# FFT convolutions of a three-stage SSM chain: the transform regrouped as 128 by 32 points, its products on 64x64 blocks

## The chip, the core and the metric

The kernel runs on one core of one Trainium2 chip. TensorE (PE) multiplies matrices into PSUM, which the kernel divides into banks of 128x512 f32; VectorE (DVE), ScalarE (ACT) and GpSimd (POOL) work elementwise; SyncE (SP) issues most of the transfers (DMAs) between main memory and SBUF. The metric is the device time of the whole launch in microseconds, lower is better. Before the change, three runs gave a median of 788.92 us, from 779.39 to 792.97.

## The reference

A sequence of 2048 positions and 512 channels passes two kinds of layers, in the order A, B, A, B, each added to its input after a layer norm. Every layer is a long causal convolution per channel, done by an FFT of length 4096.

```python
def _A_ref(q, k, v, shift_k, ssm_k, ssm_D):
    k_shift = short causal convolution of k (4 taps)
    kv = k_shift * v
    y = irfft(rfft(kv, 2 * S) * rfft(ssm_k, 2 * S))[:S]
    return q * (y + kv * ssm_D)

def _B_ref(u, log_A_real, A_imag, C_real, C_imag, log_dt, D_skip):
    A = -exp(log_A_real) + 1j * A_imag;  C = (C_real + 1j * C_imag) * dt
    K = 2.0 * einsum("dn,dnl->dl", C, exp(A * dt * arange(L))).real
    return irfft(rfft(u, 2 * L) * rfft(K, 2 * L))[:L] + u * D_skip

x = A_q
x = x + _A_ref(_layernorm(x), ...)
x = x + _B_ref(_layernorm(x), ...)
x = x + _A_ref(_layernorm(x), ...)
x = x + _B_ref(_layernorm(x), ...)
```

The block is shortened to its sense. The convolution of layer A doesn't depend on x, so it is needed once; B's filter K ("the taps") is the same in both rounds, but B's convolution runs twice.

## The kernel before, in words

Channels are handled in four quarters of 128. A 4096-point real transform is made as two passes of matrix products. `fwd_group` (L175) does the first pass (32 points over the partitions, tile pf); DVE transposes its result by 32x32 blocks into z (L193, L195). The second pass, `f2_chunk` (L200), runs over 32 frequency columns k in eight chunks of four: for each k one matmul of a 128x128 table w2[:, k] with 128 columns of z, into one PSUM bank pu of 4 x 128. An f32 matmul appears in the profile as two instructions, each with its own weight load.

`spectrum_quarter` does this for the filters (two spectra, tile zk) and stores each chunk's 128x512 result to main memory (spec; L259 copies, L260 stores). `convolution` does it for the data (zu) and multiplies by the stored spectrum. Its steps for a chunk s are: load the spectrum rows as kab[128, 2, 4, 128] by two DMAs (L274; real parts repeated in both halves of [:, 0], imaginary parts in [:, 1]); f2_chunk; ACT copies pu with its halves swapped and one negated into sw (L291, L292); DVE forms vv = pu * kab[:, 0] (L293); POOL multiplies sw by kab[:, 1] (L295); vv + sw is summed on POOL, or on DVE for every third chunk of the B rounds (L296). Some steps later (`lag`, 2 in A, 4 in B) the sum goes through the inverse product: four 128x128 matmuls with mm into a bank pi (L305), which ACT copies to ie (L306). After a quarter's eight chunks DVE transposes back (L320, tile w), the last pass L326 (tile po) gives time samples, and `finish` adds them to x.

There are three convolutions of 32 chunks each and two spectra of 32 chunks each. Stage 1 runs two generators beside each other: `stream` makes the taps K (exponentials and sines of 64 steps on ACT, products on DVE and POOL, contraction L534 on PE) and then the second spectrum, and `diagonal` makes the gated input kv (POOL and DVE), the first spectrum and convolution A. Then comes the first round of layer B, a short stage with the second gated update (`gated_update`), and the second round of B, which stores the output (L886).

Tiles come from pools with a fixed number of buffers: kab 3 in A and 4 in B, vv and sw 2 in A (NSA) and 5 in B (NSB). In stage 1 the tag c1 has three PSUM banks for pf, pu, pi and po, and the second spectrum shares two banks (pm) with the taps; in the B rounds c1 has four, and pf has banks of its own. A scheduler orders each engine's instructions when the program is built; every engine and the SP queue then work through their lists in that order, and in the built program SP's DMAs take turns on eight completion counters.

Of the kernel before, what the change touches and what calls it, by code (L numbers as in the profile page):

```python
# [21 lines left out]
CK = 4  # L22
# [10 lines left out]
def dft_constants():  # L33
    c = lambda t: np.cos(2 * np.pi * t)
    s = lambda t: np.sin(2 * np.pi * t)
    n1 = np.arange(32)
    k2 = np.arange(64)
    j = np.arange(32)
    n2 = [32 * (j // 16) + 16 * b + j % 16 for b in range(2)]
    w1 = np.zeros((2, 32, 2, 2, 32))  # L40
    w4 = np.zeros((2, 2, 32, 2, 32))
    w2 = np.zeros((32, 2, 2, 32, 2, 64))
    for b in range(2):
        w1[b, :, b, 0, 0] = 1
        w1[b, :, b, 1, 0] = (-1.0) ** n1
        w4[b, 0, 0, b] = 1 / NFFT
        w4[b, 1, 0, b] = (-1.0) ** n1 / NFFT
        m = n2[b][:, None]
        for k in range(1, 32):
            w1[b, :, b, 0, k] = c(n1 * k % 64 / 64)  # L50
            w1[b, :, b, 1, k] = -s(n1 * k % 64 / 64)
            w4[b, 0, k, b] = 2 * c(n1 * k % 64 / 64) / NFFT
            w4[b, 1, k, b] = -2 * s(n1 * k % 64 / 64) / NFFT
            ph = m * (k + 64 * k2)[None, :] % NFFT / NFFT
            w2[k, b, 0, :, 0], w2[k, b, 0, :, 1] = c(ph), -s(ph)
            w2[k, b, 1, :, 0], w2[k, b, 1, :, 1] = s(ph), c(ph)
        for q in range(32):
            ph = m[:, 0] * (64 * q) % NFFT / NFFT
            w2[0, b, 0, :, 0, q] = c(ph)
            if q > 0:  # L60
                w2[0, b, 0, :, 1, q] = -s(ph)
            ph = m[:, 0] * (32 + 64 * q) % NFFT / NFFT
            w2[0, b, 1, :, 0, 32 + q], w2[0, b, 1, :, 1, 32 + q] = c(ph), -s(ph)
        w2[0, b, 0, :, 1, 0] = (-1.0) ** m[:, 0]
    w2 = w2.reshape(32, 128, 128)
    mm = w2.transpose(0, 2, 1).copy()
    mm[0].reshape(2, 64, 128)[:, 1:] *= 2.0
    w1 = w1.reshape(64, 128)
    f = lambda a: np.ascontiguousarray(a, dtype=np.float32)
    return {  # L70
        "w1": f(np.concatenate([w1, w1])),
        "w2": f(w2.transpose(1, 0, 2)),
        "mm": f(mm.transpose(1, 0, 2)),
        "w4": f(w4.reshape(128, 64)),
    }
# [24 lines left out]
def kernel(ctx: ExitStack, tc: tile.TileContext, out, x_in, kv_in, ssmk_in, ssmd_in,  # L100
# [26 lines left out]
    LV = 0  # L127
# [12 lines left out]
    w2 = cpool.tile([128, 32, 128], F32, name="w2")  # L140
# [56 lines left out]
    def f2_chunk(z, c, first=None, tag="c1"):  # L197
        pu = bank("pu", tag).rearrange("p (k c) -> p k c", k=CK)
        for i in range(CK):
            ins = T.matmul(pu[:, i, :], w2[:, c * CK + i, :], z[:, :, c * CK + i, :], start=True, stop=True)  # L200
            if first is not None:
                after(ins, first)
        return pu, ins
# [27 lines left out]
    def spectrum_quarter(which, q, src, pool, zlast, zb, tag):  # L231
        z = pool.tile([128, 64, 32, 2], F32, name="zk", tag="z", bufs=zb)
        dr = pool.tile([1, 128], F32, name="dr", tag="dr", bufs=1)
        nc.sync.dma_start(dr, (ssmd_in, dsk_in)[which][:, 128 * q:128 * q + 128])
        for g in range(4):
            kk = pool.tile([128, 512], F32, name="kk", tag="kk", bufs=(NKK, 2)[which])
            nc.sync.dma_start(kk, src[4 * q + g])
# [12 lines left out]
        for c in range(NCH):  # L250
            pu, ins = f2_chunk(z, c, None, tag)
            if c == NCH - 1:
                zlast.append(ins)
# [5 lines left out]
            S.copy(pc, pu.rearrange("p k c -> p (k c)"))  # L259
            nc.sync.dma_start(spec[which][q][c], pc)  # L260
            yield
# [3 lines left out]
    def convolution(which, pools, steps, finish, lag, ahead, nk, ns, nw, inplace, add_dve, zlast=None, late_step=None, first_b=False):  # L265
        NS = NQ * NCH
        z, ie, todo, kabs, vvs, ws, i1s = {}, {}, {}, {}, {}, {}, {}

        def load(s):
# [3 lines left out]
            for h in range(2):  # L273
                (G if first_b and s < GL else nc.sync).dma_start(kab[64 * h:64 * h + 64].rearrange("p r k c -> p r (k c)"),  # L274
                                  spec[which][q][c].rearrange("(r k) x -> k r x", r=2))
            if c == 0:
                G.tensor_copy(kab[64:65, 0, 0, :], kab[64:65, 1, 0, :])
                G.memset(kab[64:65, 1, 0, :], 0.0)
                G.memset(kab[0:1, 1, 0, :], 0.0)
            kabs[s] = kab  # L280

        for s in range(-2 * NCH, NS + lag + NCH + 1):
# [3 lines left out]
            if 0 <= s < NS:  # L286
                q, c = divmod(s, NCH)
                pu, _ = f2_chunk(z[q](), c, i1s.get(s - ns))
                sw = pool.tile([128, CK, 128], F32, name="sw", tag="sw", bufs=ns)
                vv = pool.tile([128, CK, 128], F32, name="vv", tag="vv", bufs=ns)  # L290
                S.mul(sw[0:64], pu[64:128], -1.0)  # L291
                swapped[0] = S.copy(sw[64:128], pu[0:64])  # L292
                V.tensor_mul(vv, pu, kabs[s][:, 0])  # L293
                last = not inplace and s >= NS - LV
                (V if last else G).tensor_mul(sw, sw, kabs[s][:, 1])  # L295
                (V if last or s % add_dve == add_dve - 1 else G).tensor_add(vv, vv, sw)  # L296
                vvs[s] = vv
            t = s - lag
            if 0 <= t < NS:
# [3 lines left out]
                pi = bank("pi").rearrange("p (k c) -> p k c", k=CK)  # L303
                for i in range(CK):
                    i1s[t] = T.matmul(pi[:, i, :], mm[:, c * CK + i, :], vvs[t][:, i, :], start=True, stop=True)  # L305
                S.copy(ie[q][:, :, c * CK:(c + 1) * CK, :], pi.rearrange("p k (x r) -> p x k r", r=2))  # L306
# [299 lines left out]
    with ExitStack() as actx:  # L606
# [3 lines left out]
        NSA = 2  # L610
# [6 lines left out]
        def gated(grp, onpool):  # L617
            kvt = ap.tile([128, 39, 32], F32, name="kvt", tag="kab", bufs=NKA)
            nc.sync.dma_start(kvt.rearrange("p t c -> p (t c)"), kv_in[grp])
# [20 lines left out]
        def row_stats(t):  # L640
            xt = ap.tile([128, 512], F32, name="xt", tag="kk", bufs=NKK)
            nc.sync.dma_start(xt, x_in[:, t, :])
# [28 lines left out]
        def ln_rows(j):  # L671
            xr = ap.tile([128, 4, 512], F32, name="xr", tag="xq", bufs=1)
            nc.sync.dma_start(xr, x_in[:, 4 * j:4 * j + 4, :])
# [117 lines left out]
    NSB = 5  # L791
# [81 lines left out]
    def finish_b(rnd, q, g, po):  # L873
# [11 lines left out]
        if rnd == 1:  # L885
            nc.sync.dma_start(out[4 * q + g], yo.rearrange("p t c -> p (t c)"))  # L886
# [8 lines left out]
    ADB = 3  # L895
# [93 lines left out]
```

## Time and profile before

| | |
|---|---|
| three runs, median (lowest to highest) | 788.92 us (779.39 to 792.97) |
| span of the profiled execution | 778.6 us, 10.3 below the median, 0.8 below the fastest run |
| mean granted TensorE clock | 0.899 |
| instructions | 14526 |
| DMA packets, bytes | 89996, 148.05 MB |

No time other than its span is listed for the profiled execution. In the profile, busy time is the union of an engine's instructions; PE is the matmuls, PEld the weight loads, which may lie beside them. A group row reads: line, engine, operation, output<-inputs, shapes, count | busy us, mean ns of one | idle us of the engine just before them and what ended it. In the chain that ended last each row is a start, a length and what ran.

### The profile page before, as it was taken

The numbers are of one execution on the slowest core, as the hardware profiler recorded it, in microseconds if no ns is written. First come the engines' busy times: TensorE is split into PE (matmuls) and PEld (weight loads), VectorE is DVE, ScalarE is ACT, GpSimd is POOL, SyncE is SP. The second block draws the span as 40 slices with busy tenths as digits, with TensorE's granted clock in tenths as the row PEclk, the third lists the DMA queues.
The fourth block names the chain that finished last, engine by engine and source line by source line (L and its number), as shares of the span: only waits on it lengthen the run. The fifth ranks groups of instructions, "written<-read, shape, count | busy, mean of one in ns | idle before, by whom it ended". The sixth has DMA issues, their size and how long they took to land. (4 is left out here: it accounts for less than half of the span.)

```text
span 778.6 us, 14526 instructions
## 1 busy us (share of the span) xinstructions
PE 629.0 (81%) x5064; PEld 447.4 (57%) x5064; DVE 614.3 (79%) x1015; ACT 473.9 (61%) x849; POOL 502.1 (64%) x477
## 2 busy tenths in 40 slices
PE   2277797798888989999799998389799844799996
PEld 2154565565657665576467564276567721476673
DVE  7768989899965948959958969626568989868776
ACT  4126275356278888679566884439646618768572
POOL 5977868777666967549668664016767820388793
PEclk9678698689886989999999998699989986899999
DMA  9678178378266899685564643868977541088792
GB/s 329 241 244 298 50 243 265 101 234 287 88 198 154 262 254 262 203 247 163 167 180 105 195 171 89 259 204 197 250 175 211 142 108 54 5 197 224 202 244 104
DMA packets 89996, 148.05 MB, mean 190 GB/s; under 512 B 8892, under 2 KB 38084, under 8 KB 87364
## 3 DMA queue, kind: packets, MB, share of 16 engines
q1 hardware_dynamic: 89028, 144.71, 63.7%
q0 software_dynamic: 896, 2.43, 1.1%
q8 instruction: 40, 0.66, 0.4%
q14 instruction: 32, 0.26, 0.1%
HBM read 103.06 MB, written 44.04 MB: 189 GB/s over the span
## 5 line engine op out<-in xcount | busy, mean ns | idle before, releaser
L295 POOL TENSOR_TENSOR sw<-sw,kab 128x512 f32<-128x512 f32 x96 | 124.7, 1305 | 77.9 <-ACT sw L292 71.0
L200 PEld LDWEIGHTS pu<-zu,w 128*128 128x128 f32 x768 | 101.0, 203 | 53.0 <-issue 16.1
L200 PE MATMUL pu<-zu,w 128*128 128x128 f32 x768 | 115.8, 295 | 13.4 <-DVE vv L293 7.8
L296 POOL TENSOR_TENSOR vv<-vv,sw 128x512 f32<-128x512 f32 x76 | 100.2, 1321 | 28.5 <-DVE vv L293 25.6
L293 DVE TENSOR_TENSOR vv<-pu,kab 128x512 f32<-128x512 f32 x96 | 65.0, 680 | 63.1 <-ACT sw L292 29.3
L305 PE MATMUL pi<-vv,mm 128*128 128x128 f32 x768 | 108.6, 287 | 3.5 <-DVE vv L293 2.7
L519 POOL TENSOR_TENSOR xy<-tt,m 128x512 f32<-128x512 f32 x64 | 87.3, 1364 | 32.6 <-ACT tt L508 13.8
L305 PEld LDWEIGHTS pi<-vv,mm 128*128 128x128 f32 x768 | 97.9, 199 | 15.6 <-issue 8.8
L175 PE MATMUL pf<-kk,wz 128*128 128x256 f32 x256 | 76.8, 444 | 36.7 <-POOL kk L247 30.7
L291 ACT ACTIVATE sw<-pu 64x512 f32<-64x512 f32 x96 | 57.0, 594 | 72.3 <-PE pu L200 67.4
L200 PE MATMUL pu<-zk,w 128*128 128x128 f32 x512 | 75.8, 300 | 10.0 <-DVE zk L195 8.9
L175 PEld LDWEIGHTS pf<-kk,wz 128*128 128x128 f32 x256 | 52.9, 219 | 53.2 <-POOL kk L247 33.6
L200 PEld LDWEIGHTS pu<-zk,w 128*128 128x128 f32 x512 | 70.1, 210 | 18.8 <-DVE zk L195 11.0
L506 ACT ACTIVATE tt<-pa 128x512 f32<-128x512 f32 x64 | 38.4, 601 | 69.5 <-PE pa L498 66.4
L520 DVE TENSOR_TENSOR tt<-tt,m 128x512 f32<-128x512 f32 x64 | 70.3, 1098 | 1.8 <-ACT tt L508 1.5
L483 ACT ACTIVATE m<-pm 128x512 f32<-128x512 f32 x96 | 54.8, 603 | 25.9 <-PE pm L481 24.1
L259 ACT COPY pc<-pu 128x512 f32<-128x512 f32 x64 | 37.1, 591 | 52.6 <-PE pu L200 35.2
L534 PE MATMUL pk<-xy,tt 128*32 128x64 f32 x2048 | 52.0, 237 | 15.6 <-DVE tt L520 9.0
L534 PEld LDWEIGHTS pk<-xy,tt 128*32 128x32 f32 x2048 | 37.6, 118 | 41.1 <-issue 26.0
L326 PE MATMUL po<-w,w 128*64 128x512 f32 x192 | 53.9, 637 | 8.3 <-DVE w L320 7.6
L521 DVE SCALAR_TENSOR_TENSOR xy<-tt,m 128x256 f32<-128x256 f32 x64 | 50.9, 798 | 12.3 <-ACT tt L507 12.2
L523 POOL TENSOR_TENSOR xy<-tt,m 128x256 f32<-128x256 f32 x64 | 57.5, 898 | 0.0
(147 smaller groups left out, 1232.5 us busy)
## 6 DMA issues: line engine op xcount, KB each, us to landing
kab<-spec SPq DMA_DIRECT2D x188, 256.0 KB, 4.8
spec<-pc SPq DMA_DIRECT2D x64, 256.0 KB, 3.9
kvt<-kv_in SPq DMA_DIRECT2D x16, 624.0 KB, 7.7
kk<-ssmk_in SPq DMA_DIRECT2D x16, 256.0 KB, 2.7
xr<-x_in SPq DMA_DIRECT2D x4, 1024.0 KB, 7.9
kv_d<-u SPq DMA_DIRECT2D x16, 256.0 KB, 6.1
kdram<-ks SPq DMA_DIRECT2D x64, 64.0 KB, 3.4
kk<-kdram SPq DMA_DIRECT2D x16, 256.0 KB, 2.6
```

The lines of the kernel that those rows point to most:

```text
L175: yield T.matmul(o, w, rhs, start=True, stop=True)
L200: ins = T.matmul(pu[:, i, :], w2[:, c * CK + i, :], z[:, :, c * CK + i, :], start=True, stop=True)
L291: S.mul(sw[0:64], pu[64:128], -1.0)
L293: V.tensor_mul(vv, pu, kabs[s][:, 0])
L295: (V if last else G).tensor_mul(sw, sw, kabs[s][:, 1])
L296: (V if last or s % add_dve == add_dve - 1 else G).tensor_add(vv, vv, sw)
L305: i1s[t] = T.matmul(pi[:, i, :], mm[:, c * CK + i, :], vvs[t][:, i, :], start=True, stop=True)
L483: i = S.activation(m, pm, AF.Exp)
L519: G.tensor_mul(xy[:, :, :, 32:64], tt[:, :, :, 1:33], m1[:, :, 32:64][:, None].to_broadcast([128, 2, 8, 32]))
L520: (G if (4 * gi + k) % E2P == E2P - 1 else V).tensor_mul(e2, e2, m2[:, None].to_broadcast([128, 2, 8, 32]))
L523: (V if (4 * gi + k) % XLP == XLP - 1 else G).tensor_mul(xy[:, 0, :, 0:32], tt[:, 0, :, 0:32], m1[:, :, 0:32])
L534: T.matmul(pk[32 * i4:32 * i4 + 32, 2 * k + i, :], e2[:, r, 4 * i + i4, :], xy[:, r, 4 * i + i4, :], start=r == 0, stop=r == 1, tile_posit ...
```

## The change

The transform is split as 128 by 32 points instead of 64 by 64. Partitions are ordered anew, by (b, a, n1), so every load from the inputs and the store of the output goes through a helper `by_half` that issues two DMAs of 64 partitions. The table w2 shrinks to [128, 32, 64], two 64x64 blocks per k; mm stays [128, 32, 128] but holds two 64x64 blocks per half, one for each spectrum product. Chunks go in pairs. `f2_pair` issues 16 matmuls for two chunks, each of a 64x64 block with 128 columns, aimed with `tile_position` at the four quarters of the array: the even chunk uses the diagonal quarters, the odd chunk the others with its halves swapped. Each chunk fills one bank, so a pair holds two. `i1_pair` issues 32 matmuls for a pair: for each k, part and half one, the parts being the two products wa = pu * kab[:, 0] and wb = pu * kab[:, 1], which add up in PSUM.

So the sum L296 is no more, and the swap and sign too: ACT copies pu whole to wb (the tile named sw) and POOL multiplies it. kab is loaded by one DMA of 128 rows and four of 32 rows that swap neighbouring blocks; the copies and memsets on POOL for chunk 0 (L277 to L279) go. NSA becomes 4, NSB 6, and no product goes to DVE in place of POOL (ADB 1000).

```diff
-    w2 = cpool.tile([128, 32, 128], F32, name="w2")
+    w2 = cpool.tile([128, 32, 64], F32, name="w2")
...
-    def f2_chunk(z, c, first=None, tag="c1"):
-        pu = bank("pu", tag).rearrange("p (k c) -> p k c", k=CK)
+    def f2_pair(z, c, first=None, tag="c1"):
+        pus = [bank("pu", tag).rearrange("p (k c) -> p k c", k=CK) for _ in range(2)]
         for i in range(CK):
-            ins = T.matmul(pu[:, i, :], w2[:, c * CK + i, :], z[:, :, c * CK + i, :], start=True, stop=True)
-            if first is not None:
-                after(ins, first)
-        return pu, ins
+            for odd in range(2):
+                k = (c + odd) * CK + i
+                for h in range(2):
+                    o = h ^ odd
+                    ins = T.matmul(pus[odd][64 * o:64 * o + 64, i, :], w2[64 * h:64 * h + 64, k, :],
+                                   z[64 * h:64 * h + 64, :, k, :], start=True, stop=True,
+                                   tile_position=(64 * h, 64 * o))
+                    if first is not None:
+                        after(ins, first)
+        return pus, ins
+
+    def i1_pair(ts):
+        pis = [bank("pi").rearrange("p (k c) -> p k c", k=CK) for _ in range(2)]
+        for i in range(CK):
+            for part in range(2):
+                for odd in range(2):
+                    k, w = ts[odd]
+                    for h in range(2):
+                        o = h ^ odd
+                        ins = T.matmul(pis[odd][64 * o:64 * o + 64, i, :],
+                                       mm[64 * h:64 * h + 64, k + i, 64 * part:64 * part + 64],
+                                       w[part][64 * h:64 * h + 64, i, :], start=part == 0, stop=part == 1,
+                                       tile_position=(64 * h, 64 * o))
+        return pis, ins
+
+    def by_half(tile_, rows, store=False):
+        src = rows.rearrange("(a b n) y -> b a n y", a=2, b=2)
+        for b in range(2):
+            ends = tile_[64 * b:64 * b + 64], src[b]
+            nc.sync.dma_start(*(ends[::-1] if store else ends))
...
         for c in range(NCH):
-            pu, ins = f2_chunk(z, c, None, tag)
+            if c % 2 == 0:
+                pus, ins = f2_pair(z, c, None, tag)
+            pu = pus[c % 2]
...
-            for h in range(2):
-                (G if first_b and s < GL else nc.sync).dma_start(kab[64 * h:64 * h + 64].rearrange("p r k c -> p r (k c)"),
-                                  spec[which][q][c].rearrange("(r k) x -> k r x", r=2))
-            if c == 0:
-                G.tensor_copy(kab[64:65, 0, 0, :], kab[64:65, 1, 0, :])
-                G.memset(kab[64:65, 1, 0, :], 0.0)
-                G.memset(kab[0:1, 1, 0, :], 0.0)
+            eng = G if first_b and s < GL else nc.sync
+            rows = spec[which][q][c]
+            eng.dma_start(kab[:, 0].rearrange("p k c -> p (k c)"), rows)
+            for r in range(2):
+                for h in range(2):
+                    o = 64 * h + 32 * r
+                    eng.dma_start(kab[o:o + 32, 1].rearrange("p k c -> p (k c)"), rows[64 * h + 32 - 32 * r:64 * h + 64 - 32 * r])
...
-                S.mul(sw[0:64], pu[64:128], -1.0)
-                swapped[0] = S.copy(sw[64:128], pu[0:64])
-                V.tensor_mul(vv, pu, kabs[s][:, 0])
-                last = not inplace and s >= NS - LV
-                (V if last else G).tensor_mul(sw, sw, kabs[s][:, 1])
-                (V if last or s % add_dve == add_dve - 1 else G).tensor_add(vv, vv, sw)
-                vvs[s] = vv
+                if s % add_dve == add_dve - 1:
+                    V.tensor_mul(wb, pu, kabs[s][:, 1])
+                    swapped[0] = last
+                else:
+                    swapped[0] = S.copy(wb, pu)
+                    G.tensor_mul(wb, wb, kabs[s][:, 1])
+                V.tensor_mul(wa, pu, kabs[s][:, 0])
+                vvs[s] = (wa, wb)
...
-                for i in range(CK):
-                    i1s[t] = T.matmul(pi[:, i, :], mm[:, c * CK + i, :], vvs[t][:, i, :], start=True, stop=True)
-                S.copy(ie[q][:, :, c * CK:(c + 1) * CK, :], pi.rearrange("p k (x r) -> p x k r", r=2))
+                if c % 2 == 1:
+                    pis, i1s[t] = i1_pair([((c - 1) * CK, vvs[t - 1]), (c * CK, vvs[t])])
+                    i1s[t - 1] = i1s[t]
+                    for d, pi in enumerate(pis):
+                        k = (c - 1 + d) * CK
+                        S.copy(ie[q][:, :, k:k + CK, :], pi.rearrange("p k (x r) -> p x k r", r=2))
...
-        NSA = 2
+        NSA = 4
...
-    NSB = 5
+    NSB = 6
...
-            nc.sync.dma_start(out[4 * q + g], yo.rearrange("p t c -> p (t c)"))
+            by_half(yo.rearrange("p t c -> p (t c)"), out[4 * q + g], True)
...
-    ADB = 3
+    ADB = 1000
```

More of the change, by code (lines that the diff above doesn't have):

```diff
@@ L33, in dft_constants @@
 def dft_constants():
[L34 to L64, printed above, removed]
@@ L68, in dft_constants @@
+    for c in range(1, NCH, 2):
+        odd = slice(CK * c, CK * c + CK)
+        mm[:, :, :, odd] = mm[::-1, :, :, odd].copy()
     w1 = w1.reshape(64, 128)
@@ L71, in dft_constants @@
         "w1": f(np.concatenate([w1, w1])),
-        "w2": f(w2.transpose(1, 0, 2)),
-        "mm": f(mm.transpose(1, 0, 2)),
+        "w2": f(w2.reshape(128, 32, 64)),
+        "mm": f(mm.reshape(128, 32, 128)),
         "w4": f(w4.reshape(128, 64)),
@@ L126 @@
     NKK = 3
-    LV = 0
     TL = 1
```

60 lines of the change are left out of this document (46 added, 14 removed).

## The prediction

> **What bounds the kernel now.** I read the page's first lines, then the busy time by stretches, then the chain that ended last.
>
> ```profile
> span 778.6 us, 14526 instructions
> PE 629.0 (81%) x5064; PEld 447.4 (57%) x5064; DVE 614.3 (79%) x1015; ACT 473.9 (61%) x849; POOL 502.1 (64%) x477
> ```
>
> No engine sets the whole span; the table by stretches (us, busy PE, PEld, DVE, ACT, POOL, then granted clock and DMA share) says where each does.
>
> ```profile
> 0.00:260.00 260.00, 191.59 (x1546) 139.87 (x1546) 216.20 (x292) 130.34 (x221) 189.59 (x181) 0.82 0.66 213
> 260.00:450.00 190.00, 175.47 (x1748) 124.16 (x1748) 156.18 (x252) 141.54 (x243) 131.43 (x124) 0.97 0.70 201
> 0.00:500.00 500.00, 400.60 (x3672) 285.33 (x3672) 413.21 (x638) 300.80 (x516) 343.86 (x325) 0.88 0.66 202
> 522.00:640.00 118.00, 98.94 (x632) 71.00 (x631) 86.72 (x170) 71.28 (x132) 75.77 (x68) 0.95 0.74 185
> 674.00:779.00 105.00, 95.41 (x620) 68.94 (x620) 76.40 (x103) 63.54 (x114) 74.52 (x65) 0.97 0.68 181
> ```
>
> Stage 1 (0 to 500: taps, both spectra, convolution A) is DVE's first (216 of 260) and PE's after 260 (175 of 190). The two B convolutions are PE's: 99 of 118 and 95 of 105. There the chain of waits is matmul after matmul; its columns are start, us, what, and an f32 matmul counts as two instructions, so x8 is one chunk.
>
> ```profile
> 684.85 0.89 PE pu L200 x8
> ...
> 711.65 1.16 PE pu L200 x8
> 712.81 0.89 PE pi L305 x8
> 713.70 1.02 PE po L326 x4
> 714.72 1.09 PE pu L200 x8
> 715.81 0.89 PE pi L305 x8
> ```
>
> One chunk's four 128x128 products with 128 columns take 0.89 us, 111 ns an instruction, and 0.20 us more when the array's shape changes before them (1.09 after po).
>
> **PE: the forward product.** The change turns each chunk's 8 instructions of L200 into 16 on 64x64 blocks, aimed in turn at four quarters. Do they run beside each other? No row has quarters, but three lines have parts of the array: quarter columns (L534), half rows (L175), half columns (L326). First the PE timeline, then L534's durations (min/median/max).
>
> ```profile
> 303.22 1.10 PE L534 MATMUL pk<-xy,tt 128*32 128x64 f32 x64
> 681.74 1.13 PE L175 MATMUL pf<-u,w 64*128 64x512 f32 x4
> 713.63 1.09 PE L326 MATMUL po<-w,w 128*64 128x512 f32 x4
> L534 PE MATMUL pk<-xy,tt x2048: 216/219/317, 72.1 to 491.8; 128*32 128x64 f32 x187
> ```
>
> At 111 ns for 128 columns, 64 columns alone cost 55 ns; L534 starts one every (1.10 - 0.22)/63 = 14 ns, so four go together, weight loads included. L175 and L326 would need 4 x 444 = 1.78 us one by one and take 1.1: two go together, by rows as by columns. I therefore take 111/4 = 28 ns an instruction. A pair of chunks costs 32 x 28 = 0.89 us where it cost 16 x 111 = 1.78; the bounds are 0.89 and, if only two go together, 1.78. The inverse product (L305) becomes 64 instructions per pair, since both spectrum products go into it: 64 x 28 = 1.78 us, as before, or 3.55 if two go together. The forward product falls by 0.445 us a chunk: 32 chunks in each convolution give 14.2 us, 64 of the spectra 28.5.
>
> **The other engines.**
>
> ```profile
> L295 POOL TENSOR_TENSOR sw<-sw,kab 128x512 f32<-128x512 f32 x96 | 124.7, 1305 | 77.9 <-ACT sw L292 71.0 <-DMA kab<-spec 5.4 <-POOL kab L278 0.5
> L296 POOL TENSOR_TENSOR vv<-vv,sw 128x512 f32<-128x512 f32 x76 | 100.2, 1321 | 28.5 <-DVE vv L293 25.6
> L291 ACT ACTIVATE sw<-pu 64x512 f32<-64x512 f32 x96 | 57.0, 594 | 72.3 <-PE pu L200 67.4 <-POOL sw L295 1.7 <-issue 1.3
> L292 ACT COPY sw<-pu 64x512 f32<-64x512 f32 x96 | 55.5, 578 | 1.1
> L259 ACT COPY pc<-pu 128x512 f32<-128x512 f32 x64 | 37.1, 591 | 52.6 <-PE pu L200 35.2 <-DMA spec<-pc 13.1 <-PE pf L175 4.0
> L296 DVE TENSOR_TENSOR vv<-vv,sw 128x512 f32<-128x512 f32 x20 | 22.5, 1124 | 11.1 <-POOL sw L295 11.0
> ```
>
> All sums L296 go: 100.2 us of POOL and 22.5 of DVE. The two half copies (1.17 us) become one copy like L259's 0.59: 96 x 0.58 = 56 us of ACT. L295 and L293 stay. The latency from a chunk's product to its inverse also loses POOL's 1.3 us, so waiting for the second of a pair (one more L295) costs nothing net; each convolution's drain grows by the longer inverse, under 1 us each.
>
> **What it adds.** Five loads per kab instead of two, and every transfer from the inputs or to the output in two halves: 902 DMAs on SP instead of 540. In the built order every DMA also waits for the eighth before it, so eight are in flight. The rows: issues with KB and us to landing, then durations of an issue.
>
> ```profile
> kab<-spec SPq DMA_DIRECT2D x188, 256.0 KB, 4.8
> raw<-rows_d SPq DMA_DIRECT2D x32, 64.0 KB, 3.6
> out_dram<-yo SPq DMA_DIRECT2D x16, 256.0 KB, 4.2
> L274 SPq DMA_DIRECT2D kab<-spec x188: 573/587/1479, 208.0 to 754.2; - x188
> L237 SPq DMA_DIRECT2D kk<-ssmk_in x16: 327/333/770, 5.6 to 153.0; - x16
> L274 POOL DMA_DIRECT2D kab<-spec x4: 612/627/697, 512.8 to 514.7; - x4
> ```
>
> Issuing is cheap: plain rows cost 0.33 us, so 5 x 0.33 = 1.65 us a chunk against 2 x 0.59 = 1.17, under a period of 3.3 (105/32). The eight in flight are not. Per chunk of the last stage there are five loads (one like kab's 4.8, four like raw's 3.6) and one half store (4.2): mean 3.85 us, so 6 x 3.85/8 = 2.9 us a chunk; with 4.8 for all it is 3.6, with 3.6 for all 2.7. I take 2.9. Two chunks of the first B round are loaded from POOL's queue: 10 issues at 0.63 instead of 4, 3.8 us ahead of POOL's first product there.
>
> A pair holds two banks at once, and stage 1 has three for all of convolution A and two for the second spectrum. Below are L200's rows in stage 1 with what PE waited for there.
>
> ```profile
> L200 PE MATMUL pu<-zk,w 128*128 128x128 f32 x448 | 68.2, 304 | 9.2 <-DVE zk L195 8.1 <-ACT pc L259 0.6 <-ACT m L483 0.5
> L200 PE MATMUL pu<-zu,w 128*128 128x128 f32 x256 | 40.6, 306 | 4.5 <-ACT zu L306 2.4 <-DVE zu L195 2.1
> ```
>
> Waits for a bank to be emptied (the ACT ones) come to 3.5 us. If every one of the 64 pair groups waited for one copy and one product (0.59 + 0.68), it were 81 us; if the taps' matmuls still fill in, nothing. I take 6, near the row. Shape changes on PE rise in the built order from 462 to 514: at most 52 x 0.2 = 10 us, half of it on the path.
>
> **Sum.** Stage 1, by the L200 rows of its parts:
>
> ```profile
> L200 PE MATMUL pu<-zu,w 128*128 128x128 f32 x200 | 30.6, 297 | 3.3 <-ACT zu L306 2.4 <-DVE zu L195 0.9
> L200 PE MATMUL pu<-zk,w 128*128 128x128 f32 x96 | 13.1, 279 | 1.6 <-DVE zk L195 1.6
> L200 PE MATMUL pu<-zk,w 128*128 128x128 f32 x320 | 50.7, 314 | 6.5 <-DVE zk L195 6.5
> ```
>
> From 260 to 450 there are 296 instructions: PE loses 296 x 0.0556 = 16.4 us and lands at 159, next to DVE's 156; 14 of it counts. Before 260 it is 376 (320, and 256 - 200 of zu), 21 us; DVE is busier there, so a third, 7. DVE itself may shorten beside a quieter POOL:
>
> ```profile
> L520 DVE TENSOR_TENSOR tt<-tt,m 128x512 f32<-128x512 f32 x64 | 70.3, 1098 | 1.8 <-ACT tt L508 1.5
> 200.42 0.68 DVE L520 TENSOR_TENSOR tt<-tt,m 128x512 f32<-128x512 f32 x1
> ```
>
> The one at 200.42 took 0.68 us, the mean is 1.10: 27 us of stretch in this line. POOL drops by 32 sums (42 of 344 us, 12%); on this and its sister lines I count 6 us (bounds 0 and 27). Stage 1: 14 + 7 + 6 - 6 - 5 = 16 us off. First B convolution: 14.2, less 3.8 for POOL's issues: 10. Second: PE falls to 81 of busy, the eight in flight give 32 x 2.9 = 93 and ends of stage 2: 95, 10 off. Together 36 of the profiled 778.6. The median of the runs, 788.9, lies 10.3 above that span; I carry this offset: **753 us**.
>
> **Rivals.**
> 1. *Two by two.* If two quarters that fill one bank exclude each other, the forward product gains nothing and the inverse costs 1.78 us more a pair. In the B stages 32 pairs give 57 us on a full PE, in convolution A half of 28, less some 10 of PE's idle: +60, **849**. It decides from 148 ns per four instructions, where the 24 groups of a pair cost the old 3.55 us. For it: no row has two row halves in one bank (L175's go to two banks). Against: L326's and L534's parts share one bank and do run together. The change doing nothing it says is this case too.
> The Trainium skill, TensorEngine Tiling (Array Packing), section Gotcha 1: PSUM Pressure, says that different row tiles cannot access the same PSUM bank at the same time. The change's diagonal quarters would break that; by that rule the time would be this rival's, and no run here shows it yet.
> 2. *The eight in flight bind.* With 4.8 us for every small load, 3.6 us a chunk: the last stage becomes 115, 10 slower; the first B stage gains nothing, stage 1 its 16 less about 5 of such waits: **788**. For it: kab already lands slower (4.8) than equal bytes elsewhere. Against: four of five loads carry a quarter of its bytes.
> 3. *PE's whole relief counts.* 39 in stage 1 (704 x 0.0556), 14 and 14: 67 off, **722**. For it: every engine is relieved at once. Against: DVE's 83% of stage 1.
>
> **How the numbers follow.** Forecast 0.50 (its own range 736 to 770), two by two 0.13, eight in flight 0.22, whole relief 0.15. The range leaves out the first rival and some of the third: 720 to 792. Two per cent (773 to 805) is about what a measurement of this kernel can tell from no change: faster 0.65 (forecast and rival 3), within 0.20, slower 0.15 (rival 1, and the tail of rival 2, whose median falls inside).
>
> **What would show it.** A pair of forward products at 0.9 us and a pair of inverses at 1.8 in the chain (1.8 and 3.55: rival 1). No L296; POOL near 400 us busy, ACT near 418. SP's waits naming earlier loads, and DVE's or POOL's products waiting for kab: rival 2. Convolution A done earlier among the taps, and the B stages near 108 and 95 us. I am wrong if stage 1, relieved on PE, keeps its 500 us, or if PE's clock, 0.82 where PE is busy 74% of the time and 0.97 at 92%, drops in the later stages because PE now pauses more.

## The result, and the profile after

The changed kernel takes **1256.7 us** (median of four runs, 1246.7 to 1260.6) where the kernel before took 786.7 on the same chip (four runs, three of them those listed above): a ratio of 1.597, 95% interval 1.584 to 1.610. The forecast was 753. Each time below is the median of a kernel's executions (four; one for e1 and e3; of e6's four one took 1345 us, far from the other three), and the profile shown of the kernel before is its fastest execution, 779.4 us, so that a stage's difference from it can be up to some 7 us too large. Line numbers are those of each run's own kernel.

First the head of the page of the changed kernel and its main DMA queue (packets, MB, share of 16 engines' time).

```profile
span 1258.7 us, 21783 instructions
PE 693.5 (55%) x8648; PEld 453.6 (36%) x8648; DVE 582.5 (46%) x995; ACT 412.8 (33%) x755; POOL 389.0 (31%) x371
DMA packets 93626, 147.49 MB, mean 117 GB/s; under 512 B 12492, under 2 KB 41684, under 8 KB 90964
q1 hardware_dynamic: 92532, 143.68, 35.7%
```

No engine is busy for much more than half of the span, and the bytes (147.5 MB) are those of before. Next the table by stretches (us; busy PE, PEld, DVE, ACT, POOL; PE's granted clock as a share of full speed, DMA share, GB/s), cut at the end of the last spectrum copy, at the last vv product of round one and at the first of round two; after, then before.

```profile
0.00:942.00 942.00, 487.38 (x5346) 321.56 (x5348) 408.33 (x648) 294.69 (x512) 297.90 (x292) 0.68 0.35 112
942.00:1040.00 98.00, 81.46 (x1466) 54.83 (x1464) 60.96 (x110) 42.86 (x90) 39.57 (x32) 0.90 0.65 200
1098.00:1259.00 161.00, 92.62 (x1580) 60.94 (x1578) 62.02 (x84) 40.70 (x80) 42.18 (x34) 0.80 0.39 119
```

```profile
0.00:524.00 524.00, 420.64 (x3786) 302.90 (x3788) 420.39 (x648) 312.51 (x542) 347.27 (x333) 0.88 0.66 203
524.00:622.00 98.00, 87.55 (x564) 64.29 (x562) 71.82 (x120) 66.34 (x124) 70.42 (x62) 0.95 0.78 197
679.00:779.00 100.00, 91.00 (x602) 64.52 (x600) 71.72 (x93) 61.84 (x112) 73.55 (x65) 0.99 0.72 190
```

Stage 1 grew by 418 us and the last stage by 61. The first B convolution, which neither reads an input nor stores an output, kept its 98. So the loss lies where transfers go through `by_half`, and the DMA share of those stretches has about halved. The waits of the changed kernel (engine, line, what it waited for: us, times, longest) are for transfers. The first row is a load through `by_half`; the other two are plain transfers that share SP's list with the halves.

```profile
POOL tb L661 <- DMA kvt<-kv_in: 177.3, 15, 16.1
ACT pc L289 <- DMA spec<-pc: 174.2, 18, 47.3
POOL sw L328 <- DMA kab<-spec: 155.4, 49, 20.0
```

Last the chain that ended last in the final stage (start, us, what), and two stretches in which only halves of an output tile were on their way.

```profile
1115.02 1.91 PE pi L221 x64
1116.93 0.88 PE pu L206 x32
...
1150.86 9.21 DMA kab<-spec
1160.08 8.77 DMA out_dram<-yo
...
1177.88 8.79 DMA out_dram<-yo
```

```profile
1167.00:1169.50 2.50, 1.76 (x16) 0.52 (x12) 0.00 (x0) 0.59 (x1) 0.00 (x0) 1.00 0.12 45
1186.00:1188.00 2.00, 0.47 (x8) 0.47 (x12) 0.69 (x1) 0.00 (x0) 0.00 (x0) 0.50 0.12 45
```

A pair's products cost about what was forecast (0.88 and 1.91 us). The store of 128 KB takes 8.8 us, and a share of 0.12 is two DMA engines of sixteen. A plain kab load beside such stores took 9.21 us, where the median before was 4.8.

### The profile page after: what moved, and what is told of

Read it like the earlier page. It is cut to its first block, busy times and chain, and to the rows that moved or that the text cites. A ratio compares the mean times of both kernels' runs of the same rounds, so it can differ in the third digit from the quotient of the medians.

```text
span 1258.7 us, 21783 instructions
## 1 busy us (share of the span) xinstructions
PE 693.5 (55%) x8648; PEld 453.6 (36%) x8648; DVE 582.5 (46%) x995; ACT 412.8 (33%) x755; POOL 389.0 (31%) x371
## 3 DMA queue, kind: packets, MB, share of 16 engines
q8 instruction: 68, 1.11, 0.4%
## 5 line engine op out<-in xcount | busy, mean ns | idle before, releaser
L206 PE MATMUL pu<-zk,w 64*64 64x128 f32 x1024 | 74.3, 349 | 137.6 <-ACT pc L289 95.2
L221 PE MATMUL pi<-vv,mm 64*64 64x128 f32 x1536 | 113.5, 289 | 6.7 <-DVE vv L329 4.2
L206 PEld LDWEIGHTS pu<-zk,w 64*64 64x64 f32 x1024 | 58.0, 174 | 156.8 <-ACT pc L289 99.3
L221 PE MATMUL pi<-sw,mm 64*64 64x128 f32 x1536 | 109.7, 283 | 1.8 <-issue 1.6
L206 PE MATMUL pu<-zu,w 64*64 64x128 f32 x1536 | 90.0, 313 | 32.3 <-DVE yo L919 15.1
L206 PEld LDWEIGHTS pu<-zu,w 64*64 64x64 f32 x1536 | 72.0, 155 | 62.1 <-DVE vv L329 17.9
L221 PEld LDWEIGHTS pi<-vv,mm 64*64 64x64 f32 x1536 | 77.0, 141 | 36.9 <-issue 12.0
L327 ACT COPY sw<-pu 128x512 f32<-128x512 f32 x96 | 53.6, 590 | 97.9 <-PE pu L206 97.6
L221 PEld LDWEIGHTS pi<-sw,mm 64*64 64x64 f32 x1536 | 79.7, 141 | 4.3 <-issue 3.7
L197 DVE STREAM_TRANSPOSE zk<-pf 128x512 f32<-128x512 f32 x64 | 44.3, 703 | 67.3 <-PE pf L177 67.3
```

What stands on the lines that cost most here:

```text
L197: V.transpose(zr, both)
L206: ins = T.matmul(pus[odd][64 * o:64 * o + 64, i, :], w2[64 * h:64 * h + 64, k, :], z[64 * h:64 * h + 64, :, k, :], start=True, stop=True, ...
L221: ins = T.matmul(pis[odd][64 * o:64 * o + 64, i, :], mm[64 * h:64 * h + 64, k + i, 64 * part:64 * part + 64], w[part][64 * h:64 * h + 64, ...
L327: swapped[0] = S.copy(wb, pu)
```

## The experiments

**Theory A**: a half transfer, whose pattern in main memory is `a n y` with a = 2 outermost, runs on two engines. **Rivals**: the number of transfers (T: SP's list, eight in flight, five loads per kab); the pairs in stage 1 (Q); the built order (E). The expectations of e1 to e4 call T theory B; theory C is in e2's the two banks that a pair holds, in e3's that nothing changes. The diffs are excerpts, with `...` for lines left out; e5 to e14, e16 and e17 are built on e2.

**e1: the price of the form.** No part of the computation; 128 KB is loaded into 64 partitions, its rows described with 64 ("full"), 16, 8, 4 or 2 ("pair") as the outermost count.

```diff
+            rows = x_in.rearrange("(a b n) y -> b a n y", a=c, b=2)[0]
+            return x_in[0:64] if c == 64 else rows
...
+            nc.sync.dma_start(t[0:64], split(c))
+            nc.vector.tensor_add(keep[0:64], keep[0:64], t[0:64])
```

> This kernel leaves the whole computation out: it only loads 64 rows of 2 KB of an input, each load alone, with the source's outermost count at 64 (full), 2 (pair, the form of the changed kernel's half loads), 4, 8 and 16; then two such loads with a plain 128-row load right behind. Theory A (a transfer runs on no more engines than its outermost count): in the changed kernel's trace about 24 packets of 2 KB per us go while a half load is alone, so 64 of them take 2.7 us on top of some 2 us: full 2.3 us from issue to use, pair 4.7, four 3.3, eight 2.7, sixteen like full; two pairs 7.5 us, and the load behind them comes after that. Theory B (the number of transfers and the eight in flight, not their form): all forms within 0.3 us of each other.

Its chain (start, us, what):

```profile
43.69 2.59 DMA lonefull<-x_in
...
47.08 5.54 DMA lonepair<-x_in
...
53.43 4.04 DMA lonefour<-x_in
...
58.28 3.19 DMA loneeight<-x_in
...
62.27 2.48 DMA lonesixteen<-x_in
...
87.62 2.71 DMA twicefull<-x_in
...
91.81 7.54 DMA twicepair<-x_in
```

The same bytes take 2.5 to 2.6 us with an outermost count of 16 or 64, and 3.2, 4.0 and 5.5 us with 8, 4 and 2, these three each 0.5 to 0.8 above what A expected. Two pair-shaped halves together take 7.5 us where two plain ones take 2.7. Two stretches of the lone pair at 47.08 show why (us; busy DVE, POOL; granted clock, DMA share, GB/s): for 1.4 us nothing moves, and then two engines' worth.

```profile
47.08:48.44 1.36, 0.00 (x0) 0.00 (x0) 1.00 0.00 0
48.44:52.00 3.56, 0.00 (x0) 0.00 (x0) 1.00 0.13 37
```

Theory A holds for the transfer alone.

**e2: the change with plain transfers.** The rows are put in the order (b, a, n1) when the arrays are laid out, so that each transfer is one of 128 plain rows.

```diff
-        src = rows.rearrange("(a b n) y -> b a n y", a=2, b=2)
-        for b in range(2):
-            ends = tile_[64 * b:64 * b + 64], src[b]
-            nc.sync.dma_start(*(ends[::-1] if store else ends))
+        ends = tile_, rows
+        nc.sync.dma_start(*(ends[::-1] if store else ends))
...
```

> The changed kernel with rows laid out in its own order in main memory, so that every half load and half store is one transfer of 128 rows; quarters, pairs and the five loads per spectrum chunk stay. Theory A (the form of the half transfers): back to 730 to 790 us, the forecast without them. Theory B (the five loads and the eight transfers in flight): stays over 1000. Theory C (pairs that hold two of three banks in stage 1): stage 1 alone stays over 650 us, so over 900 in all.

842.2 us against 788.4, ratio 1.071 (1.058 to 1.083). The plain form gives back 415 of the 470 us, but 54 remain: above A's 730 to 790, far below what B and C named.

**e3: the kernel before with half transfers only**, the same helper put into it.

```diff
-            nc.sync.dma_start(kk, src[4 * q + g])
+            by_half(kk, src[4 * q + g])
...
```

> The kernel before with nothing changed but the half loads and half stores of the inputs, the taps and the output. Theory A: they alone cost most of the 470 us, 1100 to 1250 us. Theory B: 128 more transfers on a queue that has room, 790 to 830. Theory C: no change, 780 to 800.

1216.3 us (one run), within A's range: the form costs 428 us with the old products on PE.

**e4: more transfers of plain rows.** Each half becomes two transfers of 32 rows.

```diff
-            ends = tile_[64 * b:64 * b + 64], src[b]
+            for a in range(2):
+                o = 64 * b + 32 * a
+                ends = tile_[o:o + 32], src[b, a]
+                nc.sync.dma_start(*(ends[::-1] if store else ends))
```

> The changed kernel, its rows as they are, but each half transfer split into two of 32 plain rows: more transfers, none with an outermost count of 2. Theory A: the form was the cause, 750 to 830 us although there are 152 more transfers. Theory B: more transfers, so slower than the changed kernel, over 1260.

867.4 us, ratio 1.101 (1.092 to 1.110), above A's 750 to 830. Four transfers for one cost 25 us over e2's one (by the profiles 10 in stage 1 and 17 in the last stage); two of the wrong form cost 415. So it is the form that costs most, and the count a little.

The table cuts the spans as above; each cut is read from the timeline of the copies pc and of the products vv.

| us | stage 1 | first B | between | second B |
|---|---|---|---|---|
| before | 523.6 | 98.6 | 56.5 | 99.9 |
| after | 941.5 | 98.0 | 58.9 | 160.4 |
| e2 plain transfers | 587.6 | 91.5 | 58.1 | 100.0 |
| e8 spectra one chunk at a time | 570.4 | 92.6 | 58.1 | 100.3 |
| e11 forward pairs twice | 629.4 | 98.0 | 59.9 | 106.3 |
| e12 pairs kept whole | 587.0 | 95.1 | 59.2 | 101.4 |
| e13 two loads per kab | 589.9 | 78.8 | 60.0 | 91.8 |
| e16 e8 and e13 | 569.4 | 78.2 | 58.8 | 89.4 |
| e15 before, reordered | 543.8 | 98.5 | 56.5 | 100.4 |

The span of e2 is 58 us longer than that of before: 64 in stage 1, less 7 in the first B convolution, and 2 between the rounds.

**e5: pairs as atomic sections**, meant to test theory Q.

```diff
+        with tc.tile_critical():
+            for i in range(CK):
...
```

> This is e2_whole with the 16 matmuls of each forward pair and the 32 of each inverse pair kept together in PE's built list; nothing of the taps may stand between them. In e2_whole's stage 1 (0 to 565 us) the forward pairs hold PE for 102 us and the inverse pairs for 63 us, where the B stages' price (23.3 and 33.6 us for 32 chunks) would give 70 and 34. Theory Q (the pairs are cut in stage 1, so two quarters or one work where four should, and PE's relief is lost): forward 70 to 80, inverse 34 to 45, time 800 to 825. Theory T (the five loads of a kab and the SP list are what costs): PE's rows may fall, the time stays at 835 to 850.

1157.2 us. The sections bring 128 branches into PE's list, and 1645 waits where e2 has 176; the idle time of the weight loads before them:

```profile
PEld pu L207 <- issue: 231.6, 80, 11.6
PEld pi L221 <- issue: 146.3, 48, 7.8
```

Before 128 sections that is 378 us, 3 us each. The time says nothing about Q.

**e6: two loads per kab.** The swap of the rows is left out.

```diff
-            for r in range(2):
-                for h in range(2):
-                    o = 64 * h + 32 * r
-                    eng.dma_start(kab[o:o + 32, 1].rearrange("p k c -> p (k c)"), rows[64 * h + 32 - 32 * r:64 * h + 64 - 32 * r])
+            eng.dma_start(kab[:, 1].rearrange("p k c -> p (k c)"), rows)
```

> This is e2_whole with two loads of 128 rows per kab instead of one of 128 and four of 32; the second brings the rows unswapped, so the second product uses wrong rows, and its work is the same. Theory T: 96 x 3 transfers less on SP, and 790 to 810. Theory Q: SP's list was not the bound, 832 to 845.

803.0 us against 787.6, ratio 1.021 (1.013 to 1.028), within T's range: 39 us less than e2, by the profiles 14 in stage 1, 13 and 11 in the B convolutions.

**e7: the swap made at the store** (five stores per spectrum chunk, one load per kab).

```diff
+                nc.sync.dma_start(rows[o ^ 32:(o ^ 32) + 32, 1], pc[o:o + 32])
...
+            eng.dma_start(kab.rearrange("p r k c -> p r (k c)"), rows)
```

> This is e2_whole with the swap made once, when a spectrum chunk is stored (one store of 128 rows and four of 32), so that a kab is one load of 512 KB. Transfers: 64 x 5 + 96 instead of 64 + 96 x 5, 128 fewer, and none of the small ones stands ahead of a product in the B rounds. Theory T: 800 to 815, the B stages 3 to 8 us shorter each. Theory Q: 832 to 848, stage 1 unchanged or a little longer by the stores.

833.9 us, ratio 1.060 (1.051 to 1.068). Stage 1 stays near e2's (583.9), the second B convolution gains 7 and the first nothing; the time is in Q's range, not in T's. It doesn't clear the five loads, though: no wait for kab is among the largest of the B stages any more, but at the start of the first B convolution DVE's zu waits 21.5 us for a store of a spectrum chunk, now one of five, where e2 has 10.0.

**e8: the spectra's forward product one chunk at a time**, on two quarters and one bank.

```diff
-            if c % 2 == 0:
-                pus, ins = f2_pair(z, c, None, tag)
+            pu, ins = f2_one(z, c, tag)
```

> This is e2_whole with the spectra's forward product made one chunk at a time, on two quarters and into one bank, so that PE's work there is what it was before the change (0.89 us a chunk). Theory Q: the pairs gave the spectra nothing in stage 1 anyway; their forward product stays at 60 to 75 us and the time at 830 to 850. If it is the holding of two banks that costs the taps and the first pass their turn: 805 to 825. If the pairs do help there: 860 to 870.

826.1 us, ratio 1.051 (1.042 to 1.059), 16 less than e2, between what Q and the rival named. PE's forward product in stage 1 is 109.0 us of busy time as in e2 (109.3). Its two parts (us, busy, granted clock, DMA share, GB/s; spectra zk, then convolution A zu), in e2 and then in e8:

```profile
0.00:588.00 588.00, 72.55 (x1024) 0.80 0.57 180
0.00:588.00 588.00, 37.34 (x544) 0.80 0.57 180
```

```profile
0.00:570.00 570.00, 80.32 (x1024) 0.84 0.59 185
0.00:570.00 570.00, 30.18 (x538) 0.84 0.59 185
```

So the pairs saved the spectra's product only 8 us of PE (72.6 for 80.3; 75.8 before the change), where half of it was forecast, and without them there convolution A's own product took 7 us less. Why stage 1 is 17 us shorter isn't shown by this alone: the banks that became free and the new built order go together.

**e9: the taps ahead of the gated steps**, as they stood before the change.

```diff
+            if len(tapped) >= 2:
+                for i in first:
+                    after(i, tapped[-2])
```

> This is e2_whole with the gated steps (kvt) held in the built order behind the taps as they stood before the change: 12 gated operations on DVE ahead of the first tap product instead of 32 (17 before the change). Theory E (the scheduler, given other lengths, puts the gated steps first and so starts the taps 25 us late): the first tap product ends near 72 us instead of 96, stage 1 is 15 to 25 us shorter, 818 to 828. Theory T or Q alone: the order of DVE in the first 100 us is made up for later, 836 to 846.

840.8 us, ratio 1.066 (1.058 to 1.073). The first tap product ends at 76 us instead of 96, and stage 1 is only 6 us shorter. This form of theory E falls.

**e10: e7, e8 and e9 together.**

> This is e2_whole with three edits at once: the swap made when a spectrum is stored (e7_twice), the spectra's product one chunk at a time (e8_single) and the order of e9_order. If the gains add up (8, 16 and, by theory E, 20): 795 to 805; by T and Q without E: 815 to 825. Below 788 it would be faster than the kernel before.

845.7 us, ratio 1.071 (1.064 to 1.077): the gains don't add; stage 1 is 601.9. All three ideas of what it would give missed.

**e11: every forward pair issued twice.**

```diff
-        for i in range(CK):
+        for i in [i for i in range(CK) for _ in range(2)]:
```

> This is e2_whole with every forward pair issued twice into the same banks, so that PE does the forward product's old amount of work in four quarters. The prediction counted 21 us of relief of PE in stage 1 (and 10 in each B convolution). If PE's relief is worth that: stage 1 lasts 15 to 30 us longer than e2_whole's 588 (to the last copy of a spectrum chunk), the B convolutions 10 each, 875 to 895. If stage 1 isn't bound by PE (theories T, E): stage 1 within 8 us of e2_whole's, 845 to 865 by the B convolutions alone. If a busier PE keeps a higher clock (0.71 in the first 260 us of e2_whole, 0.82 before the change): clock up by 0.05 or more there and stage 1 not longer.

895.4 us, ratio 1.133 (1.127 to 1.139). Stretches of e11, then of e2:

```profile
0.00:260.00 260.00, 181.22 (x2123) 121.73 (x2127) 207.24 (x253) 96.47 (x164) 168.19 (x157) 0.78 0.56 182
```

```profile
0.00:260.00 260.00, 181.22 (x1659) 117.53 (x1659) 211.51 (x265) 103.32 (x175) 169.53 (x161) 0.71 0.58 189
```

More PE work gets a higher clock (0.78) and the same busy time there; yet stage 1 as a whole is 42 us longer. Added PE work costs, unless the new order does (e15 prices that); what relief is worth is the next question.

**e12: both chunks of a pair start together.** In e2's built list the scheduler often runs one chunk's half of a pair as soon as its bank is free and the other's later. PE's timeline of e2 (start, us, line, count) shows two halves and one whole forward pair:

```profile
436.16 1.10 PE L206 MATMUL pu<-zu,w 64*64 64x128 f32 x16
437.41 1.09 PE L206 MATMUL pu<-zu,w 64*64 64x128 f32 x16
448.60 1.11 PE L206 MATMUL pu<-zu,w 64*64 64x128 f32 x32
```

Half a pair takes as long as a whole one. The edit holds all other matmuls of a pair behind the first one of either chunk:

```diff
...
+        for i in waiting:
+            for j in leads:
+                after(i, j)
...
```

> This is e2_whole with an order between the matmuls of a pair when the program is built: the first matmul of either chunk goes ahead of all others of its pair, so that neither chunk's half runs before the other's bank is free. In the built list most inverse pairs and more forward pairs are then whole. In e2_whole's trace from 350 to 500 us half a forward pair (16 instructions) takes 1.03 us and a whole one (32) 1.12; half an inverse pair (32) 1.89 and a whole one (64) 1.91 where it is whole in the last stage. Theory Q (what is lost in stage 1 is that the pairs are cut into their two chunks): forward plus inverse in stage 1 fall from 165 us to 110 to 135, stage 1 from 588 to 555 to 575, time 808 to 830. Theory T alone: PE's rows fall, stage 1 stays within 8 us of 588 and the time at 834 to 850.

845.0 us, ratio 1.077 (1.071 to 1.082). PE's share in stage 1 (us, busy, granted clock) for pu and pi, before, e2 and e12:

```profile
0.00:524.00 524.00, 116.84 (x776) 0.88 0.66 203
0.00:524.00 524.00, 38.47 (x256) 0.88 0.66 203
```

```profile
0.00:588.00 588.00, 109.30 (x1568) 0.80 0.57 180
0.00:588.00 588.00, 62.59 (x1024) 0.80 0.57 180
```

```profile
0.00:588.00 588.00, 93.00 (x1568) 0.77 0.57 180
0.00:588.00 588.00, 46.34 (x1024) 0.77 0.57 180
```

Cutting costs PE time, as Q says: together 171.9 us in e2 against 155.3 before, and 139.3 in e12 (110 to 135 was expected). But the stage lasts as long, and its clock falls from 0.80 to 0.77. All of PE, with the other engines as in the tables above, e2 and then e12:

```profile
0.00:588.00 588.00, 461.76 (x5346) 310.06 (x5348) 422.28 (x648) 293.04 (x512) 306.10 (x292) 0.80 0.57 180
0.00:588.00 588.00, 436.96 (x5346) 279.24 (x5348) 430.15 (x648) 292.50 (x513) 303.01 (x292) 0.77 0.57 180
```

Before the change it was 420.6 us at 0.88. So in neither run was PE as a whole relieved: the matmuls that the change doesn't touch (pf, pm, pa, pk, po) took 303 us of busy time before, 328 in e2 and 333 in e12, at a lower clock each time. Q is right as to the pairs' busy time and wrong as to the stage.

**e13: two loads per kab with the right rows.** The parts of a spectrum row are interleaved (64h + 2q + r), so that one transfer of 128 rows swaps neighbours.

```diff
-        "w2": f(w2.reshape(128, 32, 64)),
+        "w2": f(w2.transpose(0, 1, 2, 3, 5, 4).reshape(128, 32, 64)),
...
+            eng.dma_start(kab[:, 1].rearrange("p k c -> p (k c)"), rows.rearrange("(m r) y -> m r y", r=2)[:, ::-1])
```

> This is e2_whole with the two parts of a spectrum row interleaved (rows 64h + 2q + r instead of 64h + 32r + q), so that the swapped rows come by one transfer of 128 rows: two loads per kab, as before the change, and the right rows. Theory T: as in e6_kab2, 798 to 810. If the swapped transfer runs on few engines or in small pieces: above 830.

819.5 us, ratio 1.044 (1.039 to 1.049), between T's range and the other. Its B stages:

```profile
590.00:669.00 79.00, 73.42 (x1426) 49.47 (x1426) 59.93 (x109) 43.14 (x90) 39.56 (x32) 0.96 0.76 249
729.00:821.00 92.00, 79.35 (x1578) 52.61 (x1576) 60.15 (x83) 39.74 (x79) 41.19 (x33) 0.98 0.64 208
```

They are 20 and 8 us shorter than before the change. The waits of e2's B stages name what stood in the way; in e13 there are no such rows among the largest. Below them are the shares of the chain in e2's last stage (737 to 838) and the small loads of kab (issue, min/median/max ns; then landing, us).

```profile
POOL sw L326 <- DMA kab<-spec: 78.3, 39, 13.2
DVE vv L327 <- DMA kab<-spec: 33.9, 23, 2.8
```

```profile
by line: SPq L307 31.8%; DMA kab<-spec 22.7%; issue 14.1%; SPq L303 7.1%; POOL sw L326 5.6%; PE pu L206 3.0%; DVE vv L327 2.8%; DMA out_dram<-yo 2.0%; PE pf L177 1.8%; POOL yo L916 1.3%; DVE zu L195 1.2%; SPq L229 1.2%; DVE yo L918 0.7%; AC
L307 SPq DMA_DIRECT2D kab<-spec x376: 302/421/1990, 172.3 to 816.6; - x188
DMA to landing us min/median/max: 2.0/2.7/6.5
```

The chain runs through SP's issuing (L307 and L303, 39%) more than through landings: from 750 to 817 us SP issues 122 transfers in 59 of the 67 us, 0.49 each, which is 2.9 us for the six of a chunk.

Stage 1 is 16 us longer than in e6 (573.6), which has the same number of transfers of the same size; the two differ in the rows that they fetch and in their built order.

**e14: e12 and e13 together.**

> This is e12_lead and e13_two_loads together. If both losses are separate (39 us by e6_kab2, 15 to 35 by theory Q): 768 to 792, level with the kernel before or faster. If the pairs kept whole wait for banks instead: 800 to 815.

820.0 us, ratio 1.047 (1.043 to 1.052), above both ranges: nothing over e13. The pairs kept whole give nothing.

**e15: the kernel before in another built order.** Its table w2 is loaded by eight transfers instead of four.

```diff
-                        nc.sync.dma_start(w2[:, 8 * i:8 * i + 8], w2_in[:, 8 * i:8 * i + 8])
+                        for j in (8 * i, 8 * i + 4):
+                            nc.sync.dma_start(w2[:, j:j + 4], w2_in[:, j:j + 4])
```

> This is the kernel before with one neutral edit: the table w2 is loaded by eight transfers of half the size instead of four. Work and bytes are the same, but the scheduler builds another order of every engine's list. It shows what a reshuffled order alone costs stage 1 (524 us to the last copy of a spectrum chunk in the kernel before). If the loss of stage 1 in the runs so far (46 to 66 us) is mostly that the old order happened to be good: 800 to 835. If orders are worth little: 780 to 795, and the loss belongs to the change's own work.

800.5 us against 782.5, ratio 1.023 (1.011 to 1.035): slower, though whether by 2% is open. Its stage 1:

```profile
0.00:544.00 544.00, 429.87 (x3786) 307.08 (x3786) 423.80 (x648) 312.47 (x541) 347.19 (x333) 0.86 0.64 196
```

Stage 1 alone is longer, by 20 us in the profiles (18 by the medians), with the same work.

**e16: e8 and e13 together.**

> This is e13_two_loads with the spectra's product one chunk at a time (e8_single). If the two gains are separate: stage 1 near 570 and the B stages as in e13_two_loads, 798 to 808. If the stage 1 of e8_single was a lucky order: 815 to 825.

797.3 us, ratio 1.021 (1.013 to 1.029), the best of the changed kernels with the right rows: still slower than before, though whether by 2% is open. The two gains add (16 and 23; together 45). Stage 1 is 46 us longer than before, the B stages 31 shorter:

```profile
0.00:569.00 569.00, 448.89 (x5338) 302.81 (x5339) 424.83 (x648) 292.54 (x510) 303.54 (x286) 0.84 0.58 185
569.00:648.00 79.00, 73.92 (x1442) 49.86 (x1434) 59.98 (x109) 43.59 (x91) 39.68 (x32) 0.96 0.77 252
706.00:796.00 90.00, 80.32 (x1584) 52.76 (x1580) 61.04 (x84) 40.42 (x80) 42.16 (x34) 0.97 0.66 212
```

**e17: e16 with another balance of the two generators.**

```diff
-        RT = 1
-        RD = 2
+        RT = 2
+        RD = 3
```

> This is e16_two_loads_single with two steps of the taps for three of the other generator, instead of one for two, so that the taps (which end 56 us after convolution A in e2_whole, 7 in the kernel before) stand earlier in the lists; the normalizer's step goes from 26 to 34. If it is the balance of the two generators that was lost: stage 1 20 to 40 us shorter than e16_two_loads_single's, 765 to 785. If the stage is bound by what both share: within 10 us of e16_two_loads_single.

805.6 us, ratio 1.032 (1.024 to 1.039). The last tap product ends at 521 us instead of 543, but convolution A's last output at 550 instead of 489. To the last spectrum copy it is 557.8 us, 12 less than in e16, and the first B convolution takes 96.2, 18 more: what one side wins the other loses.

## Why the prediction was wrong, by its own steps

- **What it adds: the transfers "in two halves".** This step failed, and it is the one that made the result. It counted transfers (902 for 540, issues, eight in flight) and took a landing time from rows of plain transfers (4.2 us for a half store). Shape was not priced. A half whose outermost count is 2 runs on two engines: 8.8 us in the chain, and 415 us (after to e2) to 428 (e3) in all. The Trainium skill, DMA: Bandwidth & Descriptors, section Why a DMA increments its semaphore by 16 and not by 1, gives the rule: the number of engines is the largest one up to 16 that divides the slowest dimension of both patterns. e1 and the shares of 0.12 and 0.13 agree with it; the prediction didn't use it.
- **The five loads per kab.** Priced at 2.9 us a chunk by landing times and eight in flight (the six landings average 3.9 us, not 3.85; the price stays). That SP's list takes 2.9 us a chunk in e2's last stage is luck: the small loads landed in 2.7 us, not 3.6, and the chain there holds more of SP's issuing (39%) than of landings (23%). "Issuing is cheap" failed: 0.49 us a transfer where 0.33 was taken. Rival 2 had the effect, products that wait for kab, but not the mechanism: the small loads didn't land in 4.8 us. From e2 to e13 the five loads cost 13 us in the first B convolution, where the sum had only POOL's issues, and 8 in the second.
- **The B convolutions, 10 us each.** In the changed kernel neither came (98.0 for 98.6, 160.4 for 99.9), in e2 7 and nothing. With the transfers of before the sign is right and the size too small together: 20 and 8 in e13, 20 and 10 in e16.
- **PE's products.** A whole forward pair took 0.88 us (0.89 forecast) and an inverse 1.91 (1.78). Rival 1 falls, and with it, for these quarters, the rule that the prediction cites from the Trainium skill, TensorEngine Tiling (Array Packing), section Gotcha 1: PSUM Pressure, that different row tiles cannot access one bank at the same time: each bank of a pair is written by two row tiles, on different partitions, and 32 instructions in 0.88 us are four in 110 ns. All four quarters on one bank, with two row tiles on the same partitions, wasn't tried.
- **Stage 1: 14 + 7 + 6 - 6 - 5 = 16 off.** This sum failed too, in sign. PE's term took it that every pair runs whole: in e2 the forward product fell from 116.8 to 109.3 us, not to half, and the inverse rose from 38.5 to 62.6. The term "6" for bank waits was looked for as idle time, but a pair that gets its banks one by one is cut, and the cost is busy time. DVE's term came to nothing: 420 us of busy time before, 422 in e2. A term was missing: the untouched matmuls took 24 us more in e2, at a clock of 0.80 for 0.88. With more pairs whole (e12) the stage kept its 587, and PE as a whole was busier than before in every run, so that no run tests "14 of it counts" as it stands. Of the signs of being wrong, "if stage 1, relieved on PE, keeps its 500 us" came in a stronger form: the stage grew. The clock dropped too, in e2 most in stage 1 and less in the B convolutions (0.91 for 0.95, 0.96 for 0.99); that pauses of PE are the cause isn't shown.
- **L296 and ACT's copies.** Right: POOL 389 us of busy time (about 400 forecast), ACT 413 (about 418).

**What stays open**: 46 of stage 1's 64 us. e8 explains 17 (one bank at a time for the spectra, or its order). A neutral edit of the kernel before cost it 20 us there, so a part may be only that the old order was a good one. Neither the kab's transfers (14 us in e6, none in e13), nor whole pairs, nor the first taps' place, nor the generators' balance brought it back. In e16 PE is busy 28 us longer in stage 1 than before (449 for 421), at a clock of 0.84 for 0.88; whether that is a cause of the longer stage or follows from it, no run shows.

## What to carry to other kernels

Price a transfer by its pattern before its count: if the outermost count on either side is 2, two engines carry it (the loads and stores here), and the same bytes in plain rows, even in more transfers, are far cheaper. Price small transfers by the issuing engine's list as well. Products on quarters of the array pay only if the whole group stands together in PE's list, and a group that needs two banks is cut where banks are short. In a stage that a scheduler orders and several engines share, don't sell one engine's relief as time: change the order of the old kernel by a neutral edit first, and see how far that alone moves it.

## What the runs showed of the hardware that was not expected

- 16 instructions on two quarters take 1.10 us, 32 on four take 1.11: an empty quarter costs as much as a full one.
- 128 KB takes 2.6, 2.5, 3.2, 4.0 and 5.5 us for outermost counts of 64, 16, 8, 4 and 2; from 64 to 2 the time only doubles, since of the 2.6 and of the 5.5 us some 1.3 pass before a byte moves.
- The granted clock went with PE's work in stage 1: 0.77 in e12, 0.80 in e2, and in the first 260 us 0.71 in e2 and 0.78 in e11 at the same 181 us of busy time. At the lower clock the untouched matmuls took longer (303 us before, 328 in e2, 333 in e12), in e12 by more than the 16 us that its pairs saved.
